# An attention kernel laid out by its own scheduler: last output block folded whole in the attention output bank, output transfers in block order, and a new table of planned costs and plan parameters

## The chip, the cores and the metric

The kernel runs on one core of one Trainium2 chip. The metric is the device time in microseconds (us) of one execution. The engines are TensorE (PE; its weight loads are listed as PEld), VectorE (DVE), ScalarE (ACT), GpSimd (POOL) and SyncE (SP), the last used here for transfers only. Each run also lists the mean granted clock of TensorE, where 1.0 is full speed.

## The reference, cut to what matters

Two attention blocks read the same 2048 x 640 input with separate weights, and a per-token gate mixes them. Both have 32 heads of 20 columns.

```python
def _A_ref(x, wqkv, wo):                       # full softmax attention
    ...                                        # q, k, v: [B, 32, 2048, 20]
    scores = jnp.einsum("bhqd,bhkd->bhqk", q, k) * Dh ** -0.5
    p = _softmax(scores, axis=-1)
    o = jnp.einsum("bhqk,bhkd->bhqd", p, v)
    return (...)(o) @ wo

def _B_ref(x, wqkv, wo):                       # local: 8 keys, distance 2
    ...

g = _sigmoid((A_x * gate_w).sum(-1, keepdims=True))
return g * _A_ref(A_x, A_wqkv, A_wo) + (1 - g) * _B_ref(A_x, B_wqkv, B_wo)
```

The exponentials of the full attention dominate: 32 heads x 2048 queries x 2048 keys, which the kernel cuts into 2048 pieces of 128 partitions by 512 columns. Such a piece is called a unit here.

## The kernel before

The Python file does not write down an instruction order. It contains a scheduler that simulates the five engines with planned durations and builds each engine's instruction list as it goes. On the chip only the order survives: each engine runs its list, held back by semaphores, as fast as it can. A planned duration is never executed; it only decides what is put where.

```python
LAT = {"pe": 0.22, "act": 0.18, "dve": 0.13, "pool": 0.15, "sp": 0.1}   # result to waiter
...
def task(self, stream, dur, fn, reads=(), writes=(), ...):
    ...
    start = self.avail[stream]
    for d in t.deps:
        start = max(start, d.end + LAT[d.stream])
    ...                       # DVE copies (port=True) and GpSimd tasks are planned not to overlap
    t.end = start + dur
    self.avail[stream] = t.end
...
mmc  = lambda n: max(n, 64) / 2400.0 + 0.004            # planned cost, matmul of n columns
dvc  = lambda n, mode=1: 0.10 + n * 1.0417e-3 / mode    # planned cost, DVE
actc = lambda n: 0.08 + n * 0.8334e-3                   # planned cost, ACT
```

The main loop goes by tiles. A tile is two or three units whose scores PE writes into PSUM banks (`score`, and a `side` bank for a third unit), and one ACT instruction turns it into exponentials. A further unit may "ride": its scores go to a spare `side` bank, and DVE makes its exponentials with integer arithmetic, one conversion out of PSUM and three shifted copies per group of up to four units.

```python
PLAN = {          # by tile number: 19 parameters of the scheduler's choices
    0: ((0.32, 0.63), 0.32, 2.5, 2.5, 0.49, -1.0, -0.1, 11.8, ...),
    ...           # 53 more rows, the last with key 720
}
...
plan = PLAN.get(s) if acting else None
if plan:
    (SLACK, XTOL, XPRIO, XLATE, DWAIT, DIDLE, DIDLE2, DTIME, DLOW, DLATE, DVE_AHEAD, DAHEAD,
     BOOST, XBOOST, RFILL, FILL, HOLD, SBP, BOFF) = plan
...
def wanted(js):                        # may a unit ride on DVE now?
    idle = max(now, ...) + 0.4 - sch.avail["dve"]
    if idle < -DWAIT:
        return None
    ...
def qk(s):                             # scores of tile s, and of the riding unit
    ...
    if rides[s]:
        t = T("dve", 0.69, lambda e: e.tensor_scalar(uD[...], side[rb], UOFF, 0.0, op0=ALU.add, op1=ALU.max), ...)
...
def gen_d(d):                          # the other three weights of a riding group
    T("pool", 0.7, lambda e: e.tensor_tensor(vS[...], vA..., vw..., ALU.mult), ...)
    for k in range(1, K):
        T("dve", 0.11 + 0.1334 * n, lambda e, ...: e.tensor_scalar(eD[...], uD[...], SHIFTS[k], None, op0=ALU.add),
          ..., port=True)
...
def filler(limit):                     # keeps PE busy where the plan sees it idle
    for j in range(4):
        ins = e.matmul(o[32 * j:32 * j + 32, :], ..., xT[:, 0, 0:512], ...)
```

At the end, the outputs of the last 512 tokens are four blocks of 128 tokens. A block's projection ("fold") is ten matmul groups that need only earlier heads and one that needs the last normalised head group. Blocks 0 and 1 are folded ahead and kept in SBUF; blocks 2 and 3 are folded shortly before the end into two PSUM banks.

```python
def gen_prefold2():
    ...
    for blk in (2, 3):
        b = yield from bank()
        yield from mm_group(b, fold_mms(side[b][:, :], blk, qs, 0, 512, True), rd, mmc(512), last=False)
        tail_bank[blk] = b
...
def tail():
    ...                                             # 640-512 columns of all four blocks
    for blk in (2, 3):                              # own matmuls, added in PSUM
        b = tail_bank[blk]
        mm(("side", b), fold_mms(side[b][:, :], blk, q, 0, 512, False), True)
    for blk in range(2):
        mm(("score", 0), fold_mms(score[0][...], blk, q, 0, 512, False), False)
    ...
    for blk in (2, 3): T("act", actc(512), ... ACTF.Copy ...)
    for blk in range(2): T("dve", dvc(512), ... ALU.add ...)
    for blk in (2, 3, 0, 1):
        T("act" if blk > 1 else "sp", 2.0, ... e.dma_start(out_v[row:row + P, :], tout[blk]), ..., dma=True)
```

## Time and profile before

| | kernel before |
|---|---|
| three executions | 832.93, 833.49 and 1873.47 us |
| span of the profiled execution | 831.5 us, clock 1.0 |
| first exponential starts / last one ends | 19.69 / 820.38 us |
| exponential tiles on ACT | 455 of 1024 columns, 270 of 1536, one of 512: 1721 units |
| units on DVE | 327 |

The one execution of 1873 us is far outside the rest and is left out of every comparison.

The lines of the page, the groups and the timeline that carry the argument stand in the prediction. Two more views of the kernel before are needed later. The first is the page's chain that ended last, shares of the span by engine: it follows the work back from the last instruction, each time to whatever released it.

```profile
ACT 44%; PE 40%; issue 13%; DVE 3%; DVEq 0%; ACTq 0%
```

The second is PE's waits: what waited, for whom, us in total, times, longest.

```profile
PE obank L464 <- DVE qabs L456: 1.2, 1, 1.2
...
PE side L562 <- DVE rQ L956: 0.7, 2, 0.5
...
PE side L562 <- DVE qkvB L858: 0.6, 3, 0.2
```

The reader is to see that DVE, though 82 % busy, hardly holds anybody up: it has 3 % of the chain, and PE's waits for it are few and short; the longest, 1.2 us, falls before the first exponential. All of PE's waits for DVE in this view add to 8.5 us.

### The profile page before, as it was taken

The numbers are of one execution on the slowest core, as the hardware profiler recorded it, in microseconds if no ns is written. First come the engines' busy times: TensorE is split into PE (matmuls) and PEld (weight loads), VectorE is DVE, ScalarE is ACT, GpSimd is POOL, SyncE is SP. The second block draws the span as 40 slices with busy tenths as digits, with TensorE's granted clock in tenths as the row PEclk, the third lists the DMA queues.
The fourth block names the chain that finished last, engine by engine and source line by source line (L and its number), as shares of the span: only waits on it lengthen the run. The fifth ranks groups of instructions, "written<-read, shape, count | busy, mean of one in ns | idle before, by whom it ended". The sixth has DMA issues, their size and how long they took to land.

```text
span 831.5 us, 29660 instructions
## 1 busy us (share of the span) xinstructions
PE 786.0 (95%) x12650; PEld 288.5 (35%) x12650; DVE 681.9 (82%) x1197; ACT 802.2 (96%) x758; POOL 133.6 (16%) x195
## 2 busy tenths in 40 slices
PE   8999999899899899999999999999989999998998
PEld 5332233333333342343234333333333333343233
DVE  7658887689788888978897898788988878988983
ACT  4999999999999999999999999999999999999995
POOL 5031014410111111011111012111101111011110
PEclk9999999999999999999999999999999999999999
DMA  9112111201111010011001011010011011000000
GB/s 311 34 30 51 40 36 34 66 5 28 30 38 33 12 42 20 13 35 34 19 21 44 14 21 35 13 42 28 11 31 29 11 31 29 24 28 18 24 6 35
DMA packets 45016, 29.15 MB, mean 35 GB/s; under 512 B 27204, under 2 KB 43684, under 8 KB 44884
## 3 DMA queue, kind: packets, MB, share of 16 engines
q1 hardware_dynamic: 44596, 26.92, 12.5%
q8 instruction: 100, 1.64, 0.8%
q10 hardware_dynamic: 288, 0.33, 0.1%
q14 instruction: 32, 0.26, 0.1%
HBM read 11.94 MB, written 2.62 MB: 18 GB/s over the span
## 4 chain that ended last, share of the span: by engine, by line
ACT 44%; PE 40%; issue 13%; DVE 3%; DVEq 0%; ACTq 0%
ACT ebuf L1563 44%; PE score L1540 12%; PE obank L1608 10%; PE side L562 9%; PE score L562 4%; PE obank L1629 1%; DVE eD L802 1%; PE score L1236 1%; PE obank L464 1%; ACT eB L919 1%; PE score L1629 0%; PE side L1629 0%; PE side L1259 0%; DVE uD L1553 0%; ACT tB L953 0%
## 5 line engine op out<-in xcount | busy, mean ns | idle before, releaser
L1563 ACT ACTIVATE ebuf<-score 128x1024 bf16<-128x1024 f32 (+1 forms) x726 | 790.7, 1232 | 9.8 <-PE score L1540 7.9
L1540 PE MATMUL score<-qT,kT 32*128 32x512 bf16 x2032 | 289.3, 384 | 33.1 <-ACT ebuf L1563 27.2
L1553 DVE TENSOR_SCALAR uD<-score 128x512 int16<-128x512 f32 x311 | 210.2, 685 | 53.7 <-PE score L1540 51.0
L802 DVE TENSOR_SCALAR eD<-uD 128x2048 int16<-128x2048 int16 (+1 forms) x246 | 170.9, 721 | 2.6 <-PE obank L1608 1.8
L1540 PEld LDWEIGHTS score<-qT,kT 32*128 32x128 bf16 x2032 | 73.0, 91 | 277.4 <-ACT ebuf L1563 142.8
L1608 PE MATMUL obank<-ebuf,vA 128*21 128x512 bf16 x1721 | 159.4, 385 | 2.1 <-ACT ebuf L1563 0.7
L562 PE MATMUL side<-xT,kvw 128*32 128x256 bf16 (+1 forms) x2440 | 100.4, 280 | 1.7 <-DVE rQ L956 0.7
L794 POOL TENSOR_TENSOR vS<-vA,vw 128x252 bf16<-128x252 bf16 x82 | 56.5, 692 | 270.3 <-PE obank L1608 229.6
L1608 PE MATMUL obank<-eD,vS 128*21 128x512 bf16 x981 | 86.6, 379 | 0.0
L562 PEld LDWEIGHTS side<-xT,kvw 128*32 128x32 bf16 x2440 | 57.4, 96 | 36.8 <-issue 20.4
L1608 PEld LDWEIGHTS obank<-ebuf,vA 128*21 128x21 bf16 x1721 | 37.8, 89 | 83.9 <-issue 72.2
L769 POOL TENSOR_TENSOR rcp<-rcp,gA 128x16 f32<-128x16 f32 x31 | 9.2, 298 | 325.9 <-DVE rcp L767 325.9
L975 DVE TENSOR_TENSOR stage<-qkvB,repB 128x1280 bf16<-128x1280 bf16 x64 | 50.7, 829 | 0.2 <-DMA repB<-eB 0.2
L874 DVE TENSOR_TENSOR stage<-qkvB 128x1280 bf16<-128x1280 bf16 x64 | 50.2, 818 | 0.2
L858 DVE CAST qkvB<-side 128x512 bf16<-128x512 f32 (+1 forms) x69 | 40.4, 594 | 9.9 <-PE side L562 9.4
L562 PE MATMUL side<-stage,ident 128*32 128x512 bf16 (+1 forms) x608 | 38.8, 348 | 0.1
L1629 PE MATMUL obank<-xT,zero 128*32 128x512 bf16 x424 | 34.8, 382 | 0.0
L775 POOL TENSOR_TENSOR oN<-oTt,rcp 128x512 bf16<-128x512 f32 x31 | 32.6, 1052 | 2.4
L1608 PE MATMUL obank<-uD,vA 128*21 128x512 bf16 x327 | 32.2, 379 | 0.0
L1608 PEld LDWEIGHTS obank<-eD,vS 128*21 128x21 bf16 x981 | 23.9, 91 | 16.0 <-issue 3.2
L562 PE MATMUL side<-woBp,oB 128*32 128x128 bf16 (+1 forms) x580 | 28.7, 293 | 0.7 <-DVE outsb L1113 0.5
L562 PE MATMUL side<-woA_d,oTd 128*32 128x128 bf16 (+1 forms) x580 | 28.8, 292 | 0.0
(178 smaller groups left out, 585.9 us busy)
## 6 DMA issues: line engine op xcount, KB each, us to landing
repB<-eB SPq DMA_DIRECT2D x128, 32.0 KB
WqP<-in_A_wqkv_dram SPq DMA_DIRECT2D x16, 160.0 KB
stage<-in_B_wqkv_dram SPq DMA_DIRECT2D x1, 2400.0 KB
oTd<-oN SPq DMA_DIRECT2D x108, 20.0 KB
qT<-dst SPq DMA_DIRECT2D x104, 20.0 KB
out_dram<-outsb SPq DMA_DIRECT2D x12, 160.0 KB
kvw<-in_A_wqkv_dram SPq DMA_DIRECT2D x2, 800.0 KB
oTd<-in_A_x_dram SPq DMA_DIRECT2D x2, 640.0 KB
```

The costliest lines, as they stand in the source:

```text
L562: ins = e.matmul(o[j:k, :], l(j) if callable(l) else l[:, j:k], r, start=(first and i == 0), stop=(last and i == n - 1), skip_group_check= ...
L775: T(en, c2, lambda e: e.tensor_tensor(oo, ii, ib, ALU.mult), reads=["rcp", "oTt"], writes=["oN0"])
L794: T("pool", 0.7, lambda e: e.tensor_tensor(vS[:, d % 2, :, :], _ap(vA, (kb * NQ + q) * 4 * DV, [[0, K - 1], [1, 4 * DV]]), _ap(vw, 0, [[1, ...
L802: T("dve", 0.11 + 0.1334 * n, lambda e, k=k, sl=sl: e.tensor_scalar(eD[:, sl % NS, 0:512 * n].bitcast(I16), uD[d % 2][:, 0:512 * n].bitcas ...
L858: t = TB(dvc(n * TOK), lambda e, o=o, i=i: e.tensor_copy(o, i), reads=[("side", b)], writes=[key])
L874: TB(dvc(CN * TOK, 2), lambda e, w=w, ks=ks: e.tensor_tensor(prodB(w), qB[:, :, :], ks, ALU.mult), reads=["qB", "kB"], writes=[("prod", w) ...
L975: TB(dvc(CN * TOK, 2), lambda e, w=w, vs=vs, rr=rr: e.tensor_tensor(prodB(w), vs, rr, ALU.mult), reads=["vB", ("repB", w4 % NR)], writes=[ ...
L1540: ins = e.matmul(o, kT[32 * j:32 * j + 32, q, kb * P:(kb + 1) * P], qT[g % NQT][32 * j:32 * j + 32, :], start=True, stop=True)
L1553: t = T("dve", 0.69, lambda e: e.tensor_scalar(uD[d % 2][:, 512 * i:512 * (i + 1)].bitcast(I16), side[rb], UOFF, 0.0, op0=ALU.add, op1=ALU ...
L1563: exps[s] = T("act", actc(512 * n), lambda e: e.activation(ebuf[s % NE][:, 0:512 * n], score[s % 2][:, 0:512 * n], ACTF.Exp, scale=LN2 / S ...
L1608: ins = e.matmul(obank[32 * j:32 * j + DV, :], v, src, start=(kb == 0), stop=(last and k >= len(lst) - 4), skip_group_check=True)
L1629: ins = e.matmul(o[32 * j:32 * j + 32, :], w[:, 32 * j:32 * j + 32] if best else w[:, :], xT[:, 0, 0:512], start=bool(best), stop=bool(bes ...
```

## The change

The intent was to measure the engines' real spacings, give them to the scheduler, search a new table of parameters with them, and shorten the end. `BALL`, a constant that paces the local attention, changed along. In the diff below the table's 54 old and 55 new rows are cut to one each.

```diff
 PLAN = {
-    0: ((0.32, 0.63), 0.32, 2.5, 2.5, 0.49, -1.0, -0.1, 11.8, 7.0, 7.2, 0.52, 0.47, 4.4, 4.0, 0.0, 0.85, 2, 5.5, 0.0),
...                                                      (53 more rows, last key 720)
+    0: ((0.41, 0.62), 0.32, 2.5, 2.5, 0.01, -1.0, -0.11, 11.8, 7.0, 7.2, 0.39, 0.47, 4.4, 2.32, 0.0, 0.85, 2, 5.5, 0.0),
...                                                      (54 more rows, last key 710)
-LAT = {"pe": 0.22, "act": 0.18, "dve": 0.13, "pool": 0.15, "sp": 0.1}
+LAT = {"pe": 0.22, "act": 0.208, "dve": 0.163, "pool": 0.15, "sp": 0.1}
...
-    dvc = lambda n, mode=1: 0.10 + n * 1.0417e-3 / mode
-    actc = lambda n: 0.08 + n * 0.8334e-3
+    dvc = lambda n, mode=1: 0.067 + n * 1.0417e-3 / mode
+    actc = lambda n: 0.052 + n * 0.8334e-3
...
-            T("dve", 0.11 + 0.1334 * n, lambda e, k=k, sl=sl: e.tensor_scalar(
+            T("dve", 0.067 + 0.1334 * n, lambda e, k=k, sl=sl: e.tensor_scalar(
...                                                      (gen_prefold2)
-        for blk in (2, 3):
-            b = yield from bank()
-            yield from mm_group(b, fold_mms(side[b][:, :], blk, qs, 0, 512, True), rd, mmc(512), last=False)
-            tail_bank[blk] = b
+        b = yield from bank()
+        yield from mm_group(b, fold_mms(side[b][:, :], 2, qs, 0, 512, True), rd, mmc(512), last=False)
+        tail_bank[2] = b
...                                                      (tail)
-        for blk in (2, 3):
-            b = tail_bank[blk]
-            mm(("side", b), fold_mms(side[b][:, :], blk, q, 0, 512, False), True)
         for blk in range(2):
             mm(("score", 0), fold_mms(score[0][:, blk * 512:(blk + 1) * 512], blk, q, 0, 512, False), False)
+        b = tail_bank[2]
+        mm(("side", b), fold_mms(side[b][:, :], 2, q, 0, 512, False), True)
+
+        def fn(e):
+            lst = fold_mms(obank[:, :], 3, None, 0, 512, True) + fold_mms(obank[:, :], 3, q, 0, 512, False)
+            for n_, (o, l, r) in enumerate(lst):
+                for j in range(0, P, 32):
+                    ins = e.matmul(o[j:j + 32, :], l(j) if callable(l) else l[:, j:j + 32], r, start=(n_ == 0),
+                                   stop=(n_ == len(lst) - 1), skip_group_check=True)
+            return ins
+
+        T("pe", 0.215 * 11, fn, reads=..., writes=["obank"], mode="col")
...
-        for blk in (2, 3):
-            b = tail_bank[blk]
-            T("act", actc(512), lambda e, b=b, blk=blk: e.activation(tcol(blk, 0, 512), side[b][:, :], ACTF.Copy), ...
+        for blk, src, key in ((2, side[tail_bank[2]], ("side", tail_bank[2])), (3, obank, "obank")):
+            T("act", actc(512), lambda e, src=src, blk=blk: e.activation(tcol(blk, 0, 512), src[:, :], ACTF.Copy), ...
...
-        for blk in (2, 3, 0, 1):
+        for blk in (0, 1, 2, 3):
...
-    BALL = 170.0
+    BALL = 160.0
...
-            t = T("dve", 0.69, lambda e: e.tensor_scalar(
+            t = T("dve", 0.61, lambda e: e.tensor_scalar(
```

## The prediction

> **What bounds the kernel now.** I read the page's busy shares first, then the groups by shape, then the waits of ScalarE (ACT), then the timeline of the last ten microseconds. The busy shares:
>
> ```profile
> PE 786.0 (95%) x12650; PEld 288.5 (35%) x12650; DVE 681.9 (82%) x1197; ACT 802.2 (96%) x758; POOL 133.6 (16%) x195
> ```
>
> ACT is full. Its work is the softmax exponential, in tiles of two or three 512-column units (ACT's groups, shapes kept apart):
>
> ```profile
> L1563 ACT ACTIVATE ebuf<-score 128x1024 bf16<-128x1024 f32 x455 | 442.7, 1071 | 5.8 <-PE score L1540 4.0 <-ACT ebuf L1563 0.6
> L1563 ACT ACTIVATE ebuf<-score 128x1536 bf16<-128x1536 f32 x270 | 380.7, 1507 | 4.1 <-PE score L1540 3.8
> ```
>
> The two busy times add to 823.4 us, more than the page's merged 790.7 for this line: consecutive records overlap. So I took the start-to-start distances from the trace. Their medians are 905 ns after a 1024-wide tile (mean 948) and 1331 ns after a 1536-wide one (mean 1345). A unit therefore costs (1331 - 905) = 426 ns and a tile 53 ns on top. The exps at full rate need 455 x 0.905 + 270 x 1.331 = 771 us, and the other 20 ACT instructions between them some 5 us, so 776. The first exp starts at 19.7 us and the last ends at 820.4, which is 800.7 us: about 24 us are lost in that stretch, nearly all as spacings above the median (455 x 43 ns + 270 x 14 ns = 23 us). They are small late starts all over the kernel; the waits view shows as idle only a third of it:
>
> ```profile
> ACT ebuf L1563 <- PE score L1540: 7.9, 20, 2.1
> ```
>
> The time of 833.5 is thus 19.7 of start, 776 of exp rate, 24 of late starts, and 13 from the last exp to the end. The other engines are not full. In the stretch 19.7 to 820.4 (busy time by stretch, all instructions; then only the filler line, which multiplies zeros or discarded data to keep PE busy):
>
> ```profile
> 19.70:820.40 800.70, 761.92 (x12375) 275.72 (x12371) 662.82 (x1154) 792.97 (x746) 121.36 (x174) 1.00 0.12 28
> ```
> ```profile
> 19.70:820.40 800.70, 61.78 (x788) 18.24 (x788) 1.00 0.12 28
> ```
>
> DVE (third busy number) has 138 us free, and up to 62 of PE's 762 recorded us is filler that can be dropped. DVE already does 327 of the 2048 exp units by an integer trick (a 512-wide conversion out of PSUM, then three shifted copies per quad):
>
> ```profile
> L1553 DVE TENSOR_SCALAR uD<-score 128x512 int16<-128x512 f32 x311 | 210.2, 685 | 53.7 <-PE score L1540 51.0
> L802 DVE TENSOR_SCALAR eD<-uD 128x2048 int16<-128x2048 int16 x243 | 169.4, 723 | 2.6 <-PE obank L1608 1.8
> ```
>
> **What the Trainium skill says.** "ScalarE: Activation LUTs", section "What ACT_TABLE_LOAD costs", gives an ACTIVATE with immediates as 186 ns + 0.833 ns per column, with some 93 ns of overlap between neighbours; that would space 1024-wide tiles by 946 ns and 1536-wide ones by 1373. The trace has 905 and 1331. The slope agrees (426/512 = 0.832), the constant is 41 ns smaller here, and the trace decides. "Perfetto Trace Analysis", section "DVE / Act Engine Instruction", says the record runs from ALU start to the acknowledged write, while the next instruction may begin prefetching before that. The trace agrees: the DVE conversion has a record of 686 ns and a median spacing of 601 ns where no idle lies between. Planning with record lengths therefore overstates occupancy. "DMA: Bandwidth & Descriptors", section "Issuing engines are not separate DMA queues", says SP's and ACT's transfers share the same DMA engines; the last transfers here are four of 160 KB with DMA nearly idle, so only issue time and landing matter.
>
> **The change, part by part.** The program is laid out by a scheduler in the kernel file that simulates engines and fixes each engine's order; on the chip that order runs under semaphores. So the change has a small direct part and a large indirect part.
>
> (1) Tail. Last lines of the timeline before:
>
> ```profile
> 821.45 1.26 PE L562 MATMUL score<-woBp,oB 128*32 128x512 bf16 x20
> ...
> 823.34 0.45 DVE L777 STREAM_TRANSPOSE oN<-oN 128x256 f32<-128x256 f32 x1
> ...
> 826.21 1.27 PE L1068 MATMUL score<-outsb,oN 128*32 128x128 bf16 x32
> ...
> 826.89 1.08 ACT L1087 ACTIVATE stage<-score 128x512 bf16<-128x512 f32 x2 [6.51 <-PE score L1068]
> 827.53 0.69 DVE L1090 TENSOR_TENSOR stage<-score,dst 128x512 bf16<-128x512 f32 x1
> ...
> 828.14 0.68 DVE L1090 TENSOR_TENSOR stage<-score,qabs 128x512 bf16<-128x512 f32 x1
> 828.25 0.97 SPq L1095 DMA_DIRECT2D out_dram<-stage  x2
> ```
>
> PE folds blocks 2 and 3 from 821.45 to about 826.2, although the normalised last head group (the transpose) is ready at 823.8. Only then come the 32 final matmuls, and everything after them. Afterwards block 2 alone stands ahead of them, so they start at 823.9 instead of 826.2. Block 3's 40 matmuls (about 2.4 us, like the pair 821.45 to 823.8) come last, with its four final ones. PE's sum is the same, so PE still ends near 827.5. What is saved lies behind it: before, DVE's three additions end at 828.82 and then comes an issue; after, DVE's additions finish about 2.3 us earlier, and the last link is one ACT copy of 597 ns, from 827.6 to 828.2, then an issue of some 0.5 us. Saved: 828.8 - 828.2 = 0.6 us. Putting transfers in block order lets 0 and 1 leave first and adds nothing. I count -0.5 us.
>
> (2) Recalibration. The planned spacing of an exp tile falls from 0.080 to 0.052 us + 0.8334 ns per column: 933 to 905 ns and 1360 to 1332 ns. The new figures are the trace's medians (905, 1331). DVE's 512-wide operation falls from 0.633 to 0.600, the conversion from 0.69 to 0.61, the copy from 0.644 to 0.601; the trace has 601, 601 and 600. Latencies grow by the same 28 and 33 ns, so an instruction's result is as late as before, only the next may start sooner. No instruction gets faster; the planner sees 725 x 0.028 = 20 us less ACT work and, at 327 x 0.089 + 243 x 0.044 = 40 us for two groups alone, much more free DVE time.
>
> (3) The new plan. With free DVE time the planner can let more units ride on DVE. One unit moved saves ACT 426 ns plus 53 ns for 1/2.4 of a tile, 0.45 us. It costs DVE 0.601 + 3 x 0.600 / 4 = 1.05 us and PE three extra matmuls. The table is keyed by tile number in tens; the last key was 720 for 726 tiles and is now 710. Weakly, that suggests 711 to 720 tiles, some 10 fewer. At 1721/726 = 2.37 units a tile that is 24 units, 24 x 0.45 = 11 us of ACT, and 25 us of DVE's 138. I have not built it, so I take half to two thirds of this, -7 us. Late starts: the old plan underrated ACT's speed, so PE was often given side work that made it late; with true spacings I estimate 24 us falling to about 19, -5 us.
>
> Sum: 833.5 - 0.5 - 7 - 5 = 821.
>
> **The rivals.** (a) PE takes over as the bound: fewer ACT microseconds but more late starts. For it: PE is 95% busy on paper and ends 20 of ACT's idle times; each tile is already spaced by PE's small delays. Against it: the 788 filler matmuls. It would leave a gain of at most 4, time 829 to 833. (b) The tighter plan has no slack for what it does not model, so orders that look good wait on the chip; for it speaks that the old pessimistic ACT figure acted as a reserve. It would give 833 to 840. (c) The free DVE time is used in full, 60 units or more, with filler dropped on PE: 60 x 0.45 = 27 us and a time near 805 to 812. DVE's idle time speaks for it; against it, 51 of the 54 us idle before the conversions wait for PE's scores, so riding is limited by what PE and the PSUM banks offer. (d) Only the tail matters and the plan is a reshuffle: 833.
>
> **Range and chances.** Two percent of 833.5 is 16.7, so faster means under 816.8. I weigh the main path and (c) for the low side, (a) and (d) for the high one: 8 in 10 between 811 and 831. Faster 0.3, within 0.68, slower 0.02: (b) alone would have to cost over 16 us, while a worse plan would hardly have been kept.
>
> **What would show it.** Right: exp tiles between 711 and 720, more than 327 conversions on DVE, unchanged medians of 905 and 1331 ns, a stretch of exps near 788 us, the 32-odd final matmuls starting right after the transpose, and a last copy on ACT. Step (3) is wrong if the counts of tiles and conversions stay; the late-start step is wrong if (mean - median) spacing stays at 43 and 14 ns; the tail step if the time from last exp to end does not fall by about half a microsecond. Rival (a) shows as fewer ACT microseconds with more waits on PE's scores. The prediction fails as a whole if the exp stretch does not shrink.

## The result, and the profile after

| | before | after |
|---|---|---|
| median of the executions in the same rounds | 833.55 us | 836.39 us |
| executions | 832.93, 833.49, 833.61 (and 1873.47) | 835.59, 836.31, 836.47, 836.72 |
| ratio (95 % interval) | | 1.0035 (1.0015 to 1.0055) |
| span of the profiled execution | 831.53 us | 834.81 us |

A ratio is the mean time of one kernel's fast runs over the mean of the other's fast runs of the same rounds, so it is not quite the ratio of the medians. All four executions of the changed kernel had a clock of 1.0. The median before is taken with the outlier; without it, it is 833.49. The changed kernel is 0.35 % slower: "same" by a 2 % rule, but outside the scatter, and 5 us above the top of the predicted range.

The lines of the changed kernel that answer to those shown in the prediction follow, view by view. First the page's busy shares:

```profile
PE 785.8 (94%) x12601; PEld 290.4 (35%) x12601; DVE 683.0 (82%) x1191; ACT 803.3 (96%) x755; POOL 138.4 (17%) x194
```

All busy sums moved by 2 us or less except GpSimd's, which rose by 5. So no work of note was taken away or added. ACT's groups, shapes kept apart:

```profile
L1572 ACT ACTIVATE ebuf<-score 128x1024 bf16<-128x1024 f32 x443 | 429.7, 1084 | 9.7 <-PE score L1549 7.9 <-PE side L563 0.2
L1572 ACT ACTIVATE ebuf<-score 128x1536 bf16<-128x1536 f32 x279 | 390.9, 1521 | 3.5 <-PE score L1549 3.1
```

There are 443 two-unit and 279 three-unit tiles (and one single), in place of 455 and 270. The tile count fell by three, from 726 to 723, but the units on ACT rose by three, from 1721 to 1724: nine tiles more have three units, twelve fewer have two. Accordingly DVE's conversions fell from 327 to 324. Idle before these tiles rose from 9.9 to 13.2 us. DVE's largest groups:

```profile
L1562 DVE TENSOR_SCALAR uD<-score 128x512 int16<-128x512 f32 x304 | 204.3, 682 | 51.2 <-PE score L1549 49.6 <-ACT g L754 0.4
L803 DVE TENSOR_SCALAR eD<-uD 128x2048 int16<-128x2048 int16 x243 | 170.2, 725 | 3.5 <-PE obank L1617 2.3
```

Then the windows view of the stretch of exponentials (length, busy PE, PEld, DVE, ACT, POOL with counts, clock, DMA share, GB/s), all instructions and then the filler line alone:

```profile
19.75:825.02 805.27, 763.00 (x12366) 278.21 (x12361) 664.50 (x1149) 793.96 (x743) 126.14 (x173) 1.00 0.11 28
```
```profile
19.75:825.02 805.27, 59.17 (x748) 16.95 (x748) 1.00 0.11 28
```

The stretch became 4.6 us longer, at unchanged speed: the medians of the start-to-start distance are 904 and 1330 ns after a two-unit and a three-unit tile (905 and 1331 before). With those two figures the whole difference can be laid out:

| us | before | after | difference |
|---|---|---|---|
| first exponential starts | 19.69 | 19.75 | +0.06 |
| tiles at full rate (two-unit x 0.905 + three-unit x 1.331) | 771.1 | 772.3 | +1.1 |
| rest of the stretch: late starts, and 20 other ACT instructions | 29.5 | 33.0 | +3.5 |
| last exponential to the end | 11.15 | 9.79 | -1.4 |
| span | 831.53 | 834.81 | +3.3 |

By the prediction's own measure, the mean distance minus the median, the late starts grew from 43 to 46 ns after a two-unit tile and from 14 to 25 ns after a three-unit tile, from 23 to 27 us in sum. So the question is where these 3.5 us or so come from, and why the tiles were not fewer. Idle that the waits view shows for the exponentials:

```profile
ACT ebuf L1572 <- PE score L1549: 11.2, 24, 2.1
```

It was 7.9 us in 20 waits. ACT waits for PE, so the next question is what PE waits for. PE's waits of the changed kernel, the largest for DVE:

```profile
PE side L563 <- DVE qkvB L859: 2.8, 8, 0.6
PE score L1549 <- DVE uD L1562: 1.8, 6, 0.5
...
PE obank L1617 <- DVE eD L803: 1.3, 2, 1.1
```

All of PE's waits for DVE now add to 16 us, against 8.5. Its waits for ACT fell, from 28.5 to 24.1. The chain that ended last agrees: DVE's share rose from 3 to 9 %.

```profile
ACT 43%; PE 34%; issue 13%; DVE 9%; SPq 1%; DMA 0%; ACTq 0%; DVEq 0%
```

One such wait in full, from the timeline of the changed kernel (start, us, engine, line, instruction; in brackets the idle time before it and who ended it), engine by engine:

```profile
62.53 6.34 POOL L821 COPY kvw<-stage 128x640 bf16<-128x640 bf16 x4
...
65.23 2.43 DVE L803 TENSOR_SCALAR eD<-uD 128x2048 int16<-128x2048 int16 x2
...
67.72 0.40 PE L1617 MATMUL obank<-ebuf,vA 128*21 128x512 bf16 x4 [1.13 <-DVE eD L803]
...
68.97 1.94 ACT L1572 ACTIVATE ebuf<-score 128x1024 bf16<-128x1024 f32 x2 [1.66 <-PE score L1549]
```

Two shifted copies take 2.43 us; at 0.68 us of record and 0.60 of spacing they would take about 1.29. GpSimd copies weights during the whole time. The batch of attention matmuls contains matmuls on the late copy, PE waits 1.13 us for it, and ACT loses 1.66 us. The Trainium skill, "SBUF — State Buffer", section "Who interferes with whom", says that DVE's two-port copies and its instructions with two SBUF inputs share a port pair with GpSimd, and that the one that comes second is blocked. The traces agree so far: I counted every DVE instruction more than 60 ns over the median of its kind, 14.0 us of excess in sum before and 20.4 after, and each of them overlaps a GpSimd instruction.

The end, from the timeline:

```profile
827.60 0.45 DVE L778 STREAM_TRANSPOSE oN<-oN 128x256 f32<-128x256 f32 x1
...
828.19 0.84 PE L1068 MATMUL score<-outsb,oN 128*32 128x128 bf16 x24 [0.89 <-DVE oN L778]
...
829.06 1.27 PE L1085 MATMUL obank<-woBp,oB 128*32 128x512 bf16 x20
...
829.86 0.68 DVE L1099 TENSOR_TENSOR stage<-score,qabs 128x512 bf16<-128x512 f32 x1
...
831.45 0.40 PE L1085 MATMUL obank<-outsb,oN 128*32 128x512 bf16 x4
831.90 0.60 ACT L1096 ACTIVATE stage<-obank 128x512 bf16<-128x512 f32 x1 [2.01 <-PE obank L1085]
```

The order is as foreseen: final matmuls right after the transpose, block 3 behind them, DVE done well before, an ACT copy last. But PE now stands still for 0.89 us until the transpose is there.

### The profile page after: what moved, and what is told of

The parts are those of the page before. It is cut to its first block, busy times and chain, and to the rows that moved or that the text cites. A ratio compares the mean times of both kernels' runs of the same rounds, so it can differ in the third digit from the quotient of the medians.

```text
span 834.8 us, 29557 instructions
## 1 busy us (share of the span) xinstructions
PE 785.8 (94%) x12601; PEld 290.4 (35%) x12601; DVE 683.0 (82%) x1191; ACT 803.3 (96%) x755; POOL 138.4 (17%) x194
## 4 chain that ended last, share of the span: by engine, by line
ACT 43%; PE 34%; issue 13%; DVE 9%; SPq 1%; DMA 0%; ACTq 0%; DVEq 0%
ACT ebuf L1572 43%; PE score L1549 10%; PE obank L1617 8%; PE side L563 7%; PE score L563 3%; DVE uD L1562 2%; DVE eD L803 2%; PE obank L1638 1%; SPq L710 1%; DVE qkvB L859 1%; DVE stage L976 1%; DVE stage L875 1%; PE score L1245 1%; PE side L891 1%; PE obank L465 1%
## 5 line engine op out<-in xcount | busy, mean ns | idle before, releaser
L1562 DVE TENSOR_SCALAR uD<-score 128x512 int16<-128x512 f32 x304 | 204.3, 682 | 51.2 <-PE score L1549 49.6
L803 DVE TENSOR_SCALAR eD<-uD 128x2048 int16<-128x2048 int16 x243 | 170.2, 725 | 3.5 <-PE obank L1617 2.3
L795 POOL TENSOR_TENSOR vS<-vA,vw 128x252 bf16<-128x252 bf16 x81 | 59.9, 741 | 270.8 <-PE obank L1617 235.2
L563 PE MATMUL side<-xT,kvw 128*32 128x256 bf16 (+1 forms) x2500 | 102.1, 280 | 1.6 <-DVE qkvB L859 1.2
L1617 PE MATMUL obank<-eD,vS 128*21 128x512 bf16 x972 | 84.0, 379 | 0.0
L875 DVE TENSOR_TENSOR stage<-qkvB 128x1280 bf16<-128x1280 bf16 x64 | 53.5, 869 | 0.1
L563 PE MATMUL side<-stage,ident 128*32 128x512 bf16 (+1 forms) x736 | 45.2, 345 | 0.3
L1617 PEld LDWEIGHTS obank<-eD,vS 128*21 128x21 bf16 x972 | 24.1, 92 | 16.8 <-issue 1.6
L764 DVE STREAM_TRANSPOSE oTt<-obank 128x512 f32<-128x512 f32 x32 | 22.7, 708 | 5.8 <-PE obank L1617 5.5
L563 PE MATMUL side<-woA_d,oTd 128*32 128x512 bf16 (+1 forms) x440 | 24.1, 308 | 0.0
```

Of the source, the lines that this page charges most:

```text
L563: ins = e.matmul(o[j:k, :], l(j) if callable(l) else l[:, j:k], r, start=(first and i == 0), stop=(last and i == n - 1), skip_group_check= ...
L795: T("pool", 0.7, lambda e: e.tensor_tensor(vS[:, d % 2, :, :], _ap(vA, (kb * NQ + q) * 4 * DV, [[0, K - 1], [1, 4 * DV]]), _ap(vw, 0, [[1, ...
L803: T("dve", 0.067 + 0.1334 * n, lambda e, k=k, sl=sl: e.tensor_scalar(eD[:, sl % NS, 0:512 * n].bitcast(I16), uD[d % 2][:, 0:512 * n].bitca ...
L875: TB(dvc(CN * TOK, 2), lambda e, w=w, ks=ks: e.tensor_tensor(prodB(w), qB[:, :, :], ks, ALU.mult), reads=["qB", "kB"], writes=[("prod", w) ...
L1562: t = T("dve", 0.61, lambda e: e.tensor_scalar(uD[d % 2][:, 512 * i:512 * (i + 1)].bitcast(I16), side[rb], UOFF, 0.0, op0=ALU.add, op1=ALU ...
L1617: ins = e.matmul(obank[32 * j:32 * j + DV, :], v, src, start=(kb == 0), stop=(last and k >= len(lst) - 4), skip_group_check=True)
```

## The experiments

The theory, as it stood once the two profiles had been compared: the table and the planned costs belong together, the new plan runs DVE with less reserve, DVE's slow instructions under GpSimd then reach PE and ACT, and the new tail is a small gain by itself. The rivals: that the new costs alone or the table alone do the harm; that PE, with its filler, is too full; that GpSimd's overlap costs both orders the same and the new order is simply another one.

Eighteen runs were made. All medians beside ratios against the kernel before, run on the same chip in the same rounds:

| run | what | median us | ratio (95 %) |
|---|---|---|---|
| e1_tail | before, with the new tail only | 832.40 | 0.9987 (0.9973 to 1.0000) |
| e7_tail_again | the same program | 832.90 | 0.9982 (0.9968 to 0.9996) |
| e4_no_tail | after, with the old tail | 836.79 | 1.0038 (1.0025 to 1.0051) |
| e2_calib | before, with the new planned costs only | 870.92 | 1.0448 (1.0433 to 1.0462) |
| e5_old_calib | after, with the old planned costs | 864.41 | 1.0370 (1.0356 to 1.0384) |
| x1_more_rides | after, more units allowed on DVE | 870.02 | 1.0432 (1.0418 to 1.0447) |
| f1_before_fill | before, filler cut to almost nothing | 844.01 | 1.0109 (1.0070 to 1.0148) |
| f2_after_fill | after, the same | 844.82 | 1.0137 (1.0113 to 1.0162) |
| p1_before_pool | before, GpSimd's work cut | 833.16 | 0.9997 (0.9982 to 1.0012) |
| p2_after_pool | after, the same | 836.10 | 1.0022 (1.0004 to 1.0041) |
| b5_before_fill5 | before, a fifth filler matmul | 860.83 | 1.0319 (1.0305 to 1.0333) |
| b6_before_pool_fill5 | the same, GpSimd's work cut | 857.57 | 1.0285 (1.0271 to 1.0299) |
| c3_after_fill5 | after, a fifth filler matmul | 860.45 | 1.0325 (1.0309 to 1.0340) |
| p3_after_pool_fill5 | the same, GpSimd's work cut | 857.78 | 1.0292 (1.0275 to 1.0309) |
| d1_before_short | before, DVE's shifted copies half as wide | 833.18 | 1.0002 (0.9986 to 1.0018) |
| d3_before_short_again | the same program | 833.04 | 0.9989 (0.9976 to 1.0003) |
| d2_after_short | after, shifted copies half as wide | 834.97 | 1.0019 (1.0004 to 1.0034) |
| d4_after_short_again | the same program | 835.16 | 1.0022 (1.0008 to 1.0036) |

### The tail alone (e1_tail, e7_tail_again)

The kernel before with the two hunks of `gen_prefold2` and `tail` of the change, and nothing else. The change of the order of the four output transfers is included, but by the code it does nothing: blocks 0 and 1 go to SP's queue and 2 and 3 to ACT's, and each queue still gets its two transfers in the same order.

```diff
 (gen_prefold2)
-        for blk in (2, 3):
+        # block 2 only
 (tail)
+        T("pe", 0.215 * 11, fn, ..., writes=["obank"], mode="col")       # block 3 whole, last
-        for blk in (2, 3, 0, 1):
+        for blk in (0, 1, 2, 3):
```

Expected of e1_tail:

> The kernel before with the change's tail alone; table, planned costs and so the order up to the last exp are those of before. Theory A (tail gains, plan loses): the exp stretch stays at about 800.7 us with 455 and 270 tiles, and the time from the last exp to the end of the span falls from 11.1 to about 9.8 us, as it is after the change: 832.2 us, 1.3 us under before. Rival (the tail is worth the predicted 0.5 us, the rest is noise of the plan): 833.0. Rival (block 3's matmuls at the end cost more than they save): 834 or more.

Expected of e7_tail_again:

> The kernel before with the new tail alone, a second time, the same program as the first of these runs: 1.1 us under before again, 832.5, if the tail is worth what its first run showed; equal to before if that was chance.

Measured: 832.40 and 832.90 us, 1.5 and 1.1 us under the medians of the kernel before in their rounds. The first interval just reaches 1, the second doesn't. At a clock of 1.0 alone the gains are 0.6 us (5 executions against 4) and 1.3 us (4 against 8). From the last exponential to the end it is 10.17 us in both profiles, against 11.15. Tiles (726) and conversions (327) are those of the kernel before. PE's and ACT's timeline of e1_tail at the end:

```profile
824.17 0.71 PE L562 MATMUL score<-woA_d,oTd 128*32 128x512 bf16 x8
824.92 1.06 PE L1067 MATMUL score<-outsb,oN 128*32 128x128 bf16 x28
...
828.17 0.40 PE L1084 MATMUL obank<-outsb,oN 128*32 128x512 bf16 x4
...
828.62 0.60 ACT L1095 ACTIVATE stage<-obank 128x512 bf16<-128x512 f32 x1 [2.01 <-PE obank L1084]
```

Here block 2's fold covers the normalisation and PE goes straight on at 824.92 (no idle in brackets), where the changed kernel waits 0.89 us. PE's own part, from the last exponential to the last matmul's end, is 7.2 us as in the kernel before (7.1). What is saved lies behind it: the last addition on DVE ended 1.34 us after PE (828.82 against 827.48), the last copy on ACT ends 0.65 us after (829.22 against 828.57), and from there to the end of the span it is 2.3 us in place of 2.7.

### The new plan with the old tail (e4_no_tail)

```diff
 (after.py, with gen_prefold2 and tail of before.py)
+        for blk in (2, 3):
+            b = yield from bank()
...
-        T("pe", 0.215 * 11, fn, ..., writes=["obank"], mode="col")
```

> The changed kernel with the old tail: new table and new planned costs. Theory A: exp stretch of about 805.3 us as after the change, then about 11.1 us to the end: 837.7 us, 4.2 us over before, so the whole loss lies in the plan. Rival (the new tail and its freed PSUM bank disturb the last tiles and carry the loss): about 833.

Measured: 836.79 us, ratio 1.0038. The stretch of exponentials is 804.7 us and the end 9.94 us. So the loss is in the plan and not in the tail; and of the 1.4 us by which the end got shorter from before to after, 1.2 come with the new plan (11.15 to 9.94) and 0.15 with the new tail (9.94 to 9.79). The new tail does little in the new plan, because the folds are finished earlier there and the normalisation is what PE waits for. The foreseen 11.1 us for this end was therefore a miss.

The same runs show how far one profile can be trusted. The stretch of e1_tail, with the order of the kernel before, is 802.55 us against 800.69, of which 1.2 us arise in the first 25 us; that of e4_no_tail, with the new order, is 804.74 against 805.27. So of the 4.6 us by which one pair differs the other shows 2.2. Late starts are from here on counted from 25 us on: each start-to-start distance above 905 or 1331 ns, with its sign. So counted, they are 22.4 us in the kernel before and 24.8 in the changed one, and 23.0 and 24.8 in e1_tail and e4_no_tail.

### Planned costs without the table, table without the costs (e2_calib, e5_old_calib)

```diff
 (e2_calib: in before.py; e5_old_calib: the reverse, in after.py)
-LAT = {"pe": 0.22, "act": 0.18, "dve": 0.13, ...}
+LAT = {"pe": 0.22, "act": 0.208, "dve": 0.163, ...}
-    dvc = lambda n, mode=1: 0.10 + ...          actc = lambda n: 0.08 + ...
+    dvc = lambda n, mode=1: 0.067 + ...         actc = lambda n: 0.052 + ...
-    0.11 + 0.1334 * n      BALL = 170.0      T("dve", 0.69, ...
+    0.067 + 0.1334 * n     BALL = 160.0      T("dve", 0.61, ...
```

Expected of e2_calib:

> The kernel before with the new planned costs alone, old table and old tail. The scheduler then makes 737 tiles and 311 units on DVE (counted in the built program). Theory A (a table fits only the costs it was searched with; planned costs by themselves bring nothing): ACT's floor rises by some 7 us and late starts grow, 845 to 860 us. Rival (better planned costs make a better order with any table, the new table spoils it): under 833.

Expected of e5_old_calib:

> The changed kernel with the old planned costs: new table, new tail; 731 tiles, 316 units on DVE. Theory A: the new table under the costs it was not searched with is as bad as the old one under the new costs, 845 to 860 us. Rival (the new table is good and the new planned costs spoil it): under 833.

Measured: 870.92 and 864.41 us. The direction was expected, the size was not. The two-unit tiles of e2_calib:

```profile
L1563 ACT ACTIVATE ebuf<-score 128x1024 bf16<-128x1024 f32 x471 | 457.0, 1073 | 19.5 <-PE score L1540 17.0 <-PE side L1540 0.5 <-PE side L562 0.3
```

and those of e5_old_calib:

```profile
L1572 ACT ACTIVATE ebuf<-score 128x1024 bf16<-128x1024 f32 x459 | 448.1, 1060 | 20.7 <-PE score L1549 18.2 <-ACT ebuf L1572 0.2
```

Idle of the two-unit tiles doubled or trebled (5.8 us in the kernel before, 9.7 in the changed one). Tiles at full rate (471 and 265 in e2_calib, 459 and 271 in e5_old_calib) need 779.0 and 776.1 us, 5 to 8 more than before, and the rest of the stretch rose to 53 and 57 us; e2_calib also has 18.8 us after its last exponential, because folds were not done in time. (Clocks of 0.991 to 0.996 added a part of it.) My reading, not tested further, is that a table of 19 parameters for every ten tiles or so fits just the sequence that it was searched on: with other costs the sequence shifts and the parameters meet other tiles. So neither part can be judged alone, and "the costs are more accurate now" says nothing of the result by itself.

A check outside the chip, with the scheduler's own arithmetic and no more than that: timed with the old planned costs, the old order ends its last exponential at 824.5 us; timed with the new planned costs, the very same old order ends it at 811.5, and the new order at 811.4. Thirteen microseconds of apparent progress are a change of yardstick. On the chip the two end at 820.4 and 825.0. The same arithmetic also says how the orders differ. Put only DVE's planned costs back to the old ones, and the old order ends at 818.0, the new one at 831.4; add 10 or 20 ns to every DVE instruction, and the old order loses 0.8 or 1.8 us, the new one 2.8 or 7.4. On paper, then, the new order leans far more on DVE being in time.

### More units on DVE (x1_more_rides)

The prediction expected its main gain from more riding units, and the change did not bring them. This run forces them, by loosening four parameters in each row of the table.

```diff
+PLAN = {k: r[:4] + (round(r[4] + 0.3, 2), round(r[5] - 0.5, 2), round(r[6] - 0.2, 2), round(r[7] - 1, 2)) + r[8:]
+        for k, r in PLAN.items()}          # DWAIT, DIDLE, DIDLE2, DTIME
```

> The changed kernel with four entries of every table row moved so that the scheduler lets more units ride on DVE: 336 in place of 324 and, counted in the built program, 748 tiles in place of 723, as a riding unit takes a PSUM bank that would have made a tile three units wide. ACT's work at full rate falls by some 4 us. The prediction's step (more units on DVE, less ACT work, shorter kernel): 830 to 834. Theory B (a ride costs a bank, tiles get narrower, and late starts grow): 845 to 860.

Measured: 870.02 us, with a wrong result (relative error 0.31) that was not planned, so the run is evidence on time only, with that reservation. ACT's groups:

```profile
L1573 ACT ACTIVATE ebuf<-score 128x1024 bf16<-128x1024 f32 x529 | 512.6, 1064 | 22.0 <-PE score L1550 19.0 <-PE side L564 0.3
L1573 ACT ACTIVATE ebuf<-score 128x1536 bf16<-128x1536 f32 x218 | 312.0, 1498 | 11.8 <-PE score L1550 10.3 <-PE side L1550 1.2
```

Units on DVE rose to 336. Yet three-unit tiles fell from 279 to 218. By the code a riding unit takes a PSUM bank that a third unit would have had; the run shows the counts, with four parameters moved at once. Full-rate work fell by only 3.4 us against the changed kernel (529 x 0.905 + 218 x 1.331 = 768.9), and the rest of the stretch rose from 33.0 to 57.6, and the end from 9.8 to 23.7. The same reservation as for e2_calib holds: the table was not searched again.

### Is PE too full? (f1_before_fill, f2_after_fill)

```diff
 (filler, in either kernel)
-            for j in range(4):
-                ins = e.matmul(o[32 * j:32 * j + 32, :], w..., xT[:, 0, 0:512], start=bool(best),
+            for j in range(1):
+                ins = e.matmul(o[32 * j:32 * j + 32, 0:32], w..., xT[:, 0, 0:32], start=bool(best),
```

Expected of f1_before_fill:

> The kernel before with each group of four filler matmuls of 512 columns cut to one of 32 columns, order unchanged, results right; some 40 of PE's 762 us in the exp stretch go. Rival R (PE's fullness makes the late starts): 3 us or more faster than before. Theory P: within 1.5 us of before, as filler stands where PE would wait anyway. If the granted clock falls, slower.

Expected of f2_after_fill:

> The same filler cut in the changed kernel. Rival R: 3 us or more faster than the changed kernel and at or under the time of before. Theory P: within 1.5 us of the changed kernel, 835 to 838.

Measured: 844.01 and 844.82 us, at mean clocks of 0.963 to 0.980. The windows view of f1_before_fill shows why (stretch, length, busy PE, PEld, DVE, ACT, POOL, clock, DMA share, GB/s):

```profile
196.60:206.80 10.20, 8.50 (x137) 3.14 (x134) 9.58 (x16) 10.20 (x11) 0.00 (x0) 1.00 0.02 6
206.80:217.00 10.20, 9.72 (x110) 3.52 (x105) 6.47 (x11) 9.21 (x8) 2.29 (x3) 0.50 0.05 12
```

After a stretch in which PE was busy 8.50 of 10.20 us the clock was halved for 10.2 us. Six such periods make 61 us in that run. Outside them and the 3 us behind each, the late starts are 30 ns a tile (19.9 us in 661 tiles), against 31 ns in the kernel before (22.4 in 721); for the changed kernel they are 33 ns without filler and 35 with it. Matched tile by tile outside these periods, the old order is 0.9 us shorter without filler and the new one 1.6. So PE's being filled up explains at most some 0.7 us of the difference between the orders. The filler pays for itself, by some 10 us in the old order and 8 in the new one.

### GpSimd's overlap (p1_before_pool, p2_after_pool)

To take away the slow DVE instructions, GpSimd's weighted values (`vS`), its normalisation (`oN`) and two thirds of its weight copies are cut to a few columns after their first use. The result is wrong on purpose (relative error 0.096); order and waits stay.

```diff
-            vS[:, d % 2, :, :], _ap(vA, ..., [[0, K - 1], [1, 4 * DV]]), _ap(vw, 0, ...), ALU.mult),
+            vS[:, d % 2, 0:K - 1 if d < 2 else 1, 0:4 * DV if d < 2 else 4], ...same sizes..., ALU.mult),
+        if 0 < g < NG - 1:                       # normalisation: 4 columns
+            ib = _ap(rcp, 0, [[4, 1], [2, 1], [1, 1], [0, 4]])
-                o = _ap(kvw, (m * CN + c) * D, [[P, CN], [32, 4], [1, 32]])
+                o = _ap(kvw, (m * CN + c) * D, [[P, CN], [32, 4], [1, 32]] if m == 2 else [[P, 1], [32, 1], [1, 4]])
```

Expected of p1_before_pool:

> The kernel before with GpSimd's large operations cut to a few columns after their first use (the scaled copies of V, the normalised heads, two thirds of the weight copies); wrong results on purpose, the order of every engine unchanged. Every DVE instruction of the kernel before that is over 60 ns slower than the median of its kind overlaps a GpSimd instruction, 14 us in sum. Theory P (GpSimd's overlaps slow DVE, DVE's lateness reaches ACT through PE): 3 to 4 us faster than before, some 830, and under 4 us of slow DVE instructions left. Rival R (late starts come from PE being full, DVE's slowness is hidden): within 1 us of before.

Expected of p2_after_pool:

> The same cut in the changed kernel, where the slow DVE instructions sum to 20 us. Theory P: 6 to 9 us faster than the changed kernel, 827 to 830, so the difference between the two kernels (2.8 us slower) vanishes or turns round. Rival R: within 1 us of the changed kernel, 836, and still slower than the other cut kernel.

Measured: the overlap is gone. The excess of slow DVE instructions fell from 14.0 to 1.8 us in the old order and from 20.4 to 1.4 in the new one. The copies of p1_before_pool, from DVE's groups, have a mean of 689 ns in place of 723:

```profile
L807 DVE TENSOR_SCALAR eD<-uD 128x2048 int16<-128x2048 int16 x243 | 161.2, 689 | 3.0 <-PE obank L1613 2.2
```

The old order gains nothing clear, as the rival had it (833.16 us, by the executions at a clock of 1.0 some 0.4 us; late starts 22.6 us, before 22.4). The new order came to 836.10, far from the 6 to 9 us that my theory expected. It was disturbed: its clock was 0.996 to 0.999, and in the profiled execution the clock was halved twice for 3.4 us:

```profile
463.60:473.80 10.20, 7.96 (x125) 2.68 (x121) 7.28 (x16) 10.20 (x12) 0.70 (x1) 1.00 0.06 17
473.80:477.20 3.40, 3.40 (x30) 0.48 (x22) 2.24 (x5) 2.46 (x4) 0.76 (x4) 0.50 0.19 50
```

Matched tile by tile with the changed kernel, p2_after_pool is 2.3 us shorter outside these two periods and the 3 us behind each, and loses 2.5 us in them; p1_before_pool, matched so with the kernel before, is 0.2 us longer. The one execution at a clock of 0.999 took 833.37 us, 2.2 us under the fastest of the changed kernel. So the times of this pair show no gain, but the traces, one of each, speak for some 2 us in the new order and none in the old one. It needed a version in which the clock cannot fall.

### The same with PE kept busier (c3_after_fill5, p3_after_pool_fill5, b5_before_fill5, b6_before_pool_fill5)

```diff
 (filler)
-            for j in range(4):
+            for j in (0, 1, 2, 3, 0):
```

Expected of c3_after_fill5, the control:

> A control for the next run: the changed kernel with five filler matmuls where it had four, order and results unchanged. In the run with GpSimd cut in the changed kernel, the TensorE clock fell to half twice for 3.4 us, at 474 and 771 us, which hides a gain; more filler is to prevent that. The filler stands where PE would wait: within 1.5 us of the changed kernel, 835 to 838, clock 1.00.

Expected of p3_after_pool_fill5, with GpSimd's work cut as above:

> GpSimd cut as before in the changed kernel, with five filler matmuls so that the clock stays up; wrong results on purpose. Theory P (slow DVE instructions under GpSimd's overlap make the new order late): 2.5 us or more under the control, 833 or less, with clock 1.00. Rival R (DVE's delays stay hidden, the new order is slower for another reason): within 1 us of the control.

Expected of b5_before_fill5 and of b6_before_pool_fill5, the same two for the old order:

> The kernel before with five filler matmuls where it had four, order and results unchanged: the control for the next run. In the changed kernel the fifth cost 24 us, some 0.12 us each for 197. If the old order's filler also reaches the end of PE's slack: 855 to 860 us.

> GpSimd cut in the kernel before with five fillers; wrong results on purpose. Theory P (only the new order is hurt by DVE's delays under GpSimd): within 1 us of its control, against 2.7 us in the changed kernel. Rival (the delays hurt both orders alike, so they do not explain the difference between the kernels): 2 to 3 us under its control.

Measured: the control missed its expectation by far. One more matmul in each of 187 groups cost 24 us (0.13 us each), and 27 us in the 197 groups of the old order. That is not a quarter more filler, as I had thought. The four matmuls of a group write four strips of 32 partitions and start within 10 ns of each other; the fifth writes the first strip again and starts 225 ns after the first (medians). The filler's recorded busy time in the stretch rises from 59.2 to 98.4 us: a group takes two slots where it took one. The two-unit tiles of c3_after_fill5:

```profile
L1572 ACT ACTIVATE ebuf<-score 128x1024 bf16<-128x1024 f32 x443 | 428.5, 1054 | 18.5 <-PE score L1549 15.5 <-PE side L563 0.3 <-PE side L1549 0.2
```

Idle before them rose from 9.7 to 18.5 us, 16.0 of it on PE. So doubling the filler is far too much: 24 of the 39 us added reach the total. With PE as the bound in this way, cutting GpSimd's work gives 2.7 us in the new order (860.45 to 857.78) and 3.3 us in the old one (860.83 to 857.57). The theory had the old order gain less than 1 us; here the rival is right, and the overlap costs both. Whether it costs them the same can't be told: b5_before_fill5 had a clock of 0.998 in three of its four executions and b6 1.0 in all, and at 1.0 alone the gains are 2.5 us in the new order (one execution against three) and 1.6 in the old one (one against four). Nor is this the state in which the two kernels run.

### DVE given time back (d1 to d4)

The last question about DVE: does the new order suffer from too little reserve there, whatever slows DVE down? After the first three, each shifted copy is made half as wide. Order, waits and planned times are unchanged. The data are then partly stale; the result still passes the comparison.

```diff
-            T("dve", 0.11 + 0.1334 * n, lambda e, k=k, sl=sl: e.tensor_scalar(
-                eD[:, sl % NS, 0:512 * n].bitcast(I16), uD[d % 2][:, 0:512 * n].bitcast(I16), ...
+            T("dve", 0.11 + 0.1334 * n, lambda e, k=k, sl=sl, W_=512 * n if sl < NS else 256 * n: e.tensor_scalar(
+                eD[:, sl % NS, 0:W_].bitcast(I16), uD[d % 2][:, 0:W_].bitcast(I16), ...
```

Expected of d1_before_short and d2_after_short:

> The kernel before with DVE's shifted copies at half their width after the first three (246 copies, about 0.3 us each taken from DVE; wrong results on purpose, order unchanged), so DVE is seldom late. From the replay of the trace, DVE's delays carry some 4 us of the kernel before: theory D (DVE lateness is a large part of the late starts) 829 to 831; rival R: within 1 us of before. If the clock falls it is told with its windows.

> The same in the changed kernel, where the replay puts 9 us on DVE's delays. Theory D: 827 to 831, so at least 5 us under the changed kernel and within 1.5 us of the other shortened kernel. Rival R: within 1 us of the changed kernel.

Expected of their repetitions:

> The kernel before with DVE's shifted copies at half width, again; only runs at clock 1.00 are compared with runs of before at clock 1.00 of the same call. Theory D (DVE's lateness hurts the new order and is hidden in the old): within 1 us of before. Rival (it hurts both alike): 2 us or more under before.

> The changed kernel with the copies at half width, again. Theory D: 2 to 3 us under the changed kernel's 836.4, 833.5 to 834.5 at clock 1.00, leaving at most 1.5 us to the other shortened kernel. Rival: within 1 us of 836.4, or the same gain in both shortened kernels, which leaves the difference of 2.9 us in place.

Measured: the copies' mean fell from 723 to 450 ns, which over 240 copies gives back 65 us of DVE time. From DVE's groups of d3_before_short_again:

```profile
L802 DVE TENSOR_SCALAR eD<-uD 128x1024 int16<-128x1024 int16 x240 | 102.1, 450 | 6.5 <-PE obank L1608 5.6
```

By medians the old order is at 833.18 and 833.04 us and the new one at 834.97 and 835.16. Since several executions had a lower clock, I compare those at a clock of 1.0 alone. The old order: mean 832.97 (4 executions), against 833.57 for the kernel before (11): 0.6 us gained. The new order: mean 834.43 (5 executions), against 836.27 for the changed kernel (4, from the result's own rounds): 1.8 us gained. The distance between the two orders shrinks from 2.7 to 1.5 us. The profiles at clock 1.0 agree in kind: PE's waits for DVE fell from 16.0 to 13.3 us in the new order and stayed at 8.5 and 8.3 in the old one; late starts fell from 24.8 to 23.2, and from 22.4 to 21.8. So about 1.2 us of the distance is DVE's thin reserve. That figure rests on few executions, and partly on a comparison across calls; from their scatter, its 95 % interval is some 0.9 us either way. My expectations (a replay of the trace with each DVE delay taken out, 4 and 9 us) were missed by far in both orders; of the repetitions, the old order's came in, and the new order's gain fell between theory and rival.

## Why the prediction was wrong, point by point

**The bound** was read rightly. ACT's exponentials at 905 and 1331 ns set the rate in both kernels.

**Step (1), the tail.** Right in its mechanism: PE's sum unchanged, the final matmuls right behind the transpose, an ACT copy as the last link, transfer order without effect. The term was somewhat small: 0.5 us were predicted; the tail alone brought 1.0 us in both profiles, and 1.5 and 1.1 by medians, whose intervals hold 0.5 as well. The part from PE's end to the last computed value was well estimated (0.6 predicted, 1.34 - 0.65 = 0.7 measured); not counted was that the end comes 2.3 instead of 2.7 us after that value. In the new plan the tail's own effect shrinks to 0.15 us in the profiles, since PE now waits for the normalisation.

**Step (2), the new costs.** The figures are right (save that DVE's planned relief is 37 us and not 40: the conversion went to 0.61, not 0.601), and the chip's own spacing did not change (904 and 1330). Wrong is the unspoken conclusion that a planner which sees 20 us less ACT work will find some of it. The semaphores already ran the old order at the true speed; with one yardstick both orders are equally long (811.5 and 811.4 us in the scheduler's arithmetic). There was no time on the ACT side to be uncovered.

**Step (3), "-7 us", is the step that failed first.** It read the last key of the table, 710 instead of 720, as fewer tiles through more riding units. The tiles did get fewer, 723, but by wider ones, and the riding units fell from 327 to 324: 1.1 us more full-rate work instead of 7 less. The working of a moved unit (0.45 us of ACT for 1.05 us of DVE) left out what it takes of PSUM: in x1_more_rides twelve more riding units than in the changed kernel went with 61 fewer three-unit tiles. That DVE's 138 free microseconds were not for sale was visible in the very line that the prediction put under a rival: 51 of 54 us idle before the conversions wait for PE's scores.

**The late starts, "24 to 19", failed with the sign reversed.** Counted as the prediction counted them, 23 us became 27. The reason given was that the old plan underrated ACT. It did, but it also overrated DVE, by some 40 us as the prediction itself computed, and as far as the runs speak that was no error to be harvested but a reserve, in which DVE's slow instructions stayed unseen. PE's waits for DVE doubled, and giving DVE its time back removes 1.2 us of the distance between the orders. Rival (b), "The tighter plan has no slack for what it does not model", had the right mechanism in part, and its range of 833 to 840 holds the result. It was given too little weight: I judged it by the 16 us that would make the kernel slower by over 2 %, not by whether it would cancel the gain, and trusted that a worse plan would hardly have been kept.

**What stays open.** The cause is shown in part only. DVE's reserve is worth 1.2 us by the times, and without GpSimd's overlap the trace is 2.3 us shorter; both relieve DVE, so the two figures may overlap and must not be added. PE's fullness is nearly excluded by f1 and f2. The kept traces tell where the growth sits: from 25 us on, the late starts behind three-unit tiles rose from 2.6 to 5.6 us, those behind two-unit tiles stayed at 19.7 and 19.3. They are few: 15 starts late by over 60 ns sum to 5.2 us, against nine with 1.8 before; e4_no_tail and e1_tail, the same orders profiled again, have the same 15 and nine, with 5.2 and 1.9 us. And they hardly yield when DVE is relieved (4.8 us in d4_after_short_again, 4.9 in p2_after_pool); what these two runs save lies mostly behind two-unit tiles. The largest, 0.82 us, ends at 293.20 us in the timeline of the changed kernel:

```profile
290.57 0.61 PE L563 MATMUL side<-woA_d,oTd 128*32 128x512 bf16 x8
...
291.52 0.61 PE L1617 MATMUL obank<-ebuf,vA 128*21 128x512 bf16 x8
...
292.50 0.82 PE L1549 MATMUL score<-qT,kT 32*128 32x512 bf16 x6
...
293.20 1.02 ACT L1572 ACTIVATE ebuf<-score 128x1024 bf16<-128x1024 f32 x1 [0.69 <-PE score L1549]
```

From 290.57 on PE was busy without a pause with a fold, filler and attention matmuls, and only then turned to the scores. So the growth itself looks like the order on PE, and DVE's relief makes up for a part of it elsewhere. No run moved that work on PE, so this is read from traces and not shown by a test. I could not take it apart further, because table and costs cannot be separated without making both worse.

**The best version** of those run is the old plan with the new tail, 832.40 and 832.90 us against 833.92 and 834.03 in the same rounds.

## What to carry to other kernels

When a planned order is replaced by one planned with better figures, time the old order with the new figures first: only what is left of the difference can be a gain. An overrated cost of an engine that others wait for can be a reserve, and taking it out should be counted as a possible cost (here about 1 us). Free time of an engine is for sale only where its input (here PE's scores and a PSUM bank) is free as well; and a direct gain at the end, however small, is best shipped by itself.

## What the Trainium skill lacked or had wrong

- "ScalarE: Activation LUTs", section "What ACT_TABLE_LOAD costs": an estimate from its constants spaces neighbouring activations of 1024 and 1536 columns by 946 and 1373 ns; for these exponentials, which read PSUM, the runs show medians of 905 and 1331 before, 904 and 1330 after, which is 41 to 43 ns less. The slope per column agrees. The point is on this section's constants alone.
- "TensorE: Matmul & The Clock Gate", section "Why this matters for your kernels", advises against PE-idle gaps above about 3 us. Here the clock was halved after 10.2 us in which PE was recorded busy for 7.96 us (and for 8.50 in another run), so that no gap in them can have reached 3 us. The page also knows drops from many short pauses, but a rule by share of activity is missing. The length of the halved periods, 3.4 and 10.2 us, agrees with the page's window of about 3.4 us and a multiple of it.
- "SBUF — State Buffer", section "Who interferes with whom": right as far as the traces go (every slow DVE instruction overlapped a GpSimd one), but it gives no measure of what that costs a kernel. Tile by tile and away from the halved clock, removing the 14.0 and 20.4 us of excess on DVE was worth nothing in the old order and 2.3 us in the new one, one trace each.
- No page has how closely filler matmuls must be dosed: 187 groups of four cost at most some 1.6 us (the tile-by-tile figure above) and held the clock; a fifth matmul in each, which makes a group take two slots, cost 24 us.
